# Parking split weights in DRAM as one float32 and splitting them again when they return

## The chip, the core and the metric

One core of a Trainium2 chip runs the kernel; the other cores are not used. The core has TensorE (PE in the profile) for matrix products, VectorE (DVE), ScalarE (ACT) and GpSimd (POOL) for element-wise work, and SyncE (SP), which here issues nearly all DMAs. Each engine takes its instructions strictly in the order in which the program lists them and waits on semaphores where an operand is not ready. Data lie in DRAM, in SBUF (128 partitions) and in PSUM, where TensorE accumulates.

The metric is the device time of one execution in microseconds (us), lower is better. It is measured several times for each kernel, and the median is quoted.

## The reference

A block-sparse attention is followed by a feed-forward layer with softplus:

```python
# q, k, v: (4, 8, 768, 64); w_in: (512, 2048); w_out: (2048, 512); blocks of 32 keys
scores = q @ k.T / sqrt(D)                       # only sampled, neighbour, first and last blocks
attn = softmax(where(mask, scores, -1e9)) @ v
x = attn.transpose(0, 2, 1, 3).reshape(3072, 512)
h = x @ w_in
g = np.maximum(h, 0.0) + np.log1p(np.exp(-np.abs(h)))
out = (g @ w_out).astype(np.float32)
```

The feed-forward weights come as 64-bit floats. The kernel turns each into a float32 with integer work, then into two parts in the `fp32r` format that TensorE multiplies at speed: a high part (the value rounded to that format) and a low part (value minus high part). A product then takes three matmuls: high by high, high by low, low by high.

## The kernel before

The hidden dimension of 2048 is cut into 16 pieces f of 128, and the 3072 tokens into 8 tiles t of 384. One iteration n of the feed-forward works on one pair (t, f). `hidden(n)` runs twelve matmuls of 384 columns into a PSUM tile `h` (lines 235 to 237). ScalarE makes |h| and its exponential (L239, L240), VectorE three steps on `u` and `e` (L246, L248, L249), ScalarE the logarithm (L254), VectorE adds (L259), ScalarE casts the high part `gh` (L263) and VectorE subtracts for the low part `gl` (L269). `project` then runs nine matmuls of 512 columns (L291 to L293), three iterations after the `hidden` of the same n (`LEAD = 3`). Tiles `gh`, `gl`, `e`, `u` have two buffers each.

The work has two phases. In phase 0 the attention runs, and the feed-forward of the first five pieces (`EARLY = 5`, 40 iterations) is spread among its steps; each result goes to DRAM (`yD`), and so does the attention's output, split in two parts (`xD`). In phase 1 the attention is over, and the other eleven pieces run for all tiles (88 iterations); x comes back from `xD`, the partial sums from `yD`.

The weights are converted during phase 0 by the class `Weights`. Its 32 halves are the 16 pieces of `w_in` (which = 0) and of `w_out` (which = 1). `tick()` advances a software pipeline; half number h takes a stage when the tick count is 4h plus the stage's number: load of the raw 64-bit data (SP, L146), magnitude (ACT, L153), last places (ACT, L157), clamp and shift (DVE, L163, L170), assemble (DVE L176, then a POOL addition L180), `high` at 10 (ACT cast, L189), `low` at 12 (DVE subtraction, L193), and `park`: the high part at 12 and the low part at 14. `convert()` calls `tick` between the attention's pieces, at one tick a piece at first and later at half a tick a piece.

The ten halves of the first five pieces stay in SBUF. The other 22 don't fit beside the attention: they are "parked", each as two DRAM tiles of 256 KB (`wD`, L198). When the attention's last piece is done, its SBUF is released and `load_w2` (L893) brings all 44 tiles back through the SP queue, two pieces of the hidden dimension per iteration.

The order on SP is the order of the source. ScalarE, VectorE, GpSimd and TensorE get their order from a list scheduler, which may pull an instruction ahead of its place in the source. At most eight DMAs of the hardware queues are outstanding: each issue first waits for the eighth before it. A load that waits on SP thus holds everything that was listed after it on SP.

Of the kernel before, what the change touches and what calls it, by code (L numbers as in the profile page):

```python
# [8 lines left out]
F32 = mybir.dt.float32  # L9
F32R = mybir.dt.float32r  # L10
# [5 lines left out]
ALU = mybir.AluOpType  # L16
# [11 lines left out]
EARLY = 5  # L28
# [3 lines left out]
LEAD = 3  # L32
# [3 lines left out]
START = 4  # L36

SPREAD = 2

WARM = 50  # L40

# [7 lines left out]
def sparse_attention_ffn(  # L49
# [22 lines left out]
    nc = tc.nc  # L72
    B, NG, P, NP, NI, _ = q.shape
# [4 lines left out]
    NT, DM = out.shape  # L78
    NF = w_in.shape[0]
# [15 lines left out]
    dram = ctx.enter_context(tc.tile_pool(name="dram", bufs=1, space=bass.MemoryType.DRAM))  # L95
# [5 lines left out]
    w1 = ctx.enter_context(tc.tile_pool(name="w1", bufs=1, side="right"))  # L101
    pools = {}
# [5 lines left out]
    xD = [dram.tile([P, 2, NC, TB], F32, name=f"xD{t}") for t in range(NTB)]  # L108
    yD = [dram.tile([P, DM], F32, name=f"yD{n}") for n in range(len(order))]
    wD = {  # L110
        (which, f): [dram.tile([P, DM], F32, name=f"wD{x}{which}{f}") for x in range(2)]
        for f in range(EARLY, NF) for which in range(2)
    }

# [1 line left out]
    W = {}  # L116
    mark = {}

    class Weights:
# [61 lines left out]

        def high(self, h):
            f, which = self.halves[h]
            if f < EARLY:
                W[which, f] = [w1.tile([P, DM], F32R, name=f"w{x}{which}{f}") for x in range(2)]
            else:
                hi = pools["conv"].tile([P, DM], F32R, tag="wh", name=f"wh{which}{f}", bufs=2)
                W[which, f] = [hi, self.t[h].bitcast(F32R)]
            tc.keep_in_program_order(nc.scalar.copy(out=W[which, f][0], in_=self.t[h]))  # L189

        def low(self, h):
            hi, lo = W[self.halves[h][::-1]]
            nc.vector.tensor_tensor(out=lo, in0=self.t[h], in1=hi.bitcast(F32), op=ALU.subtract)  # L193

        def park(self, x, h):
            f, which = self.halves[h]
            if f >= EARLY:
                nc.sync.dma_start(out=wD[which, f][x], in_=W[which, f][x].bitcast(F32))  # L198

        def tick(self):  # L200
            for stage, at in (
                (lambda h: self.park(0, h), 12), (lambda h: self.park(1, h), 14),
                (self.load, 6 - 4 * self.bufs),
                (self.low, 12), (self.high, 10),
                (self.assemble, 3), (self.shift, 2), (self.clamp, 1),
                (self.last_places, 1), (self.magnitude, 0),
            ):
                h, rest = divmod(self.at - at, 4)
                if rest == 0 and 0 <= h < len(self.halves):
                    stage(h)  # L210
            self.at += 1

        def done(self):
            return self.at > 4 * (len(self.halves) - 1) + 14


    X, E, U, L, G, po = {}, {}, {}, {}, {}, {}
# [6 lines left out]
    def load_x(t):  # L224
        x_tile(1, t)
        nc.sync.dma_start(out=X[1, t].bitcast(F32), in_=xD[t])
# [45 lines left out]
    def first_half(j):  # L272
        for stage, n in ((high, j - 2), (logarithm, j - 1), (hidden, j)):
            if 0 <= n < len(seq):
                stage(n)

    def second_half(j):
        for stage, n in ((softplus, j - 1), (low, j - 2), (rounding, j), (project, j - LEAD)):
            if 0 <= n < len(seq):
                stage(n)  # L280
# [18 lines left out]
    def load_y(t):  # L299
        for m in range(GROUPS):  # L300
            Y[t, m] = gp.tile([P, DM], F32, tag="os", name=f"y{t}_{m}", bufs=3)
            nc.sync.dma_start(out=Y[t, m], in_=yD[t * GROUPS + m])
# [49 lines left out]
    for rows in (slice(0, NR * BLOCK), slice(NR * BLOCK, P)):  # L352
# [4 lines left out]
        out=vbuf[0][:, 0, 0, :], out_offset=None, in_=v,  # L357
# [158 lines left out]
    def load_values(m):  # L516
# [18 lines left out]
        if g < 2:  # L535

            for c, lo in enumerate((b * S, (b + 1) * S - BLOCK)):
                i1 = i0 if c == 0 else 0
                if m < SPREAD:
                    if i1 == 0:  # L540
# [311 lines left out]
    def attend():  # L852
        nonlocal done
        attention[done]()
        done += 1
        gather()
        convert()

    SECOND = NTB * EARLY
# [3 lines left out]
    def convert():  # L863

        nonlocal owed
        if done < START:
            return
        owed += EARLY_TICKS if weights.at < 4 * len(early) + 9 else LATE_TICKS
        while owed >= 1 and not weights.done():
            weights.tick()  # L870
            owed -= 1
            if weights.at == 4 * weights.extra + 2:
                extractx.close()
                pools["kv2"] = kv2.enter_context(tc.tile_pool(name="kv2", bufs=1))
# [4 lines left out]
    def due(x):  # L879

        last, at = 0.0, needs[0]
        for t in range(1, NTB):
            end = t * EARLY - AHEAD
            if x <= end:
                return at + (needs[t] - at) * (x - last) / (end - last)
            last, at = end, needs[t]
        return len(attention)

    def load_w2(f):
        for which in range(2):  # L890
            W[which, f] = [pools["w2"].tile([P, DM], F32R, name=f"w{x}{which}{f}") for x in range(2)]
            for x in range(2):
                nc.sync.dma_start(out=W[which, f][x].bitcast(F32), in_=wD[which, f][x])  # L893

    ahead = None
    for j in range(len(seq) + LEAD):
        if j >= SECOND:
            t, f = seq[j][1:] if j < len(seq) else (NTB, -1)
            if f == EARLY + 2 and t + 1 < NTB:
                load_x(t + 1)  # L900
            if f == EARLY + 4:
                load_y(t)
        if j == SECOND - 3:
            load_x(0)
        first_half(j)
        while done < len(attention) and done < due(j + 0.5):
            attend()
        convert()
        second_half(j)
        while done < len(attention) and done < due(j + 1.0):  # L910
            attend()
        convert()
        if done == len(attention) and ahead is None:
            assert weights.done(), weights.at
            actx.close()
            kv2.close()
            pools["w2"] = ctx.enter_context(tc.tile_pool(name="w2", bufs=1, side="right"))
            ahead = EARLY
        while ahead is not None and ahead < min(NF, EARLY + 2 * (j + EARLY - SECOND + 1)):
            load_w2(ahead)  # L920
            ahead += 1


_BLOCKS = 24
# [35 lines left out]
```

## Time and profile before

| | |
|---|---|
| median of 3 runs | 853.09 us (847.7, 853.09, 854.35) |
| the profiled execution's own time | 850.83 us |
| span of its profile | 848.8 us |
| last store of the attention's output (start of the issue on SP) | 444.20 us |
| DMA traffic | HBM read 104.14 MB, written 36.70 MB |
| granted TensorE clock, mean | 0.975 |

The span is the time from the first to the last instruction that the profile shows; the 2 us beside it are start and end of the execution. The attention and phase 0 take about the first 444 us, phase 1 the rest. In the page's rows an engine's busy time is the union of its instructions; a line such as `L189 ACT CAST wh<-wt x22: 601/609/636` gives the source line, the engine, the operation, output and input tile, the count and the shortest, median and longest duration in ns. In a timeline row, square brackets give the time for which the engine sat idle before the instruction and what it waited for. In a row of windows, the stretch is followed by its length and by the busy time of each engine with the count of instructions, then the granted clock, the busy share of the DMA engines and their GB/s.

### The profile page before, as it was taken

How to read it: one execution, taken by the hardware profiler on the slowest of the kernel's cores; microseconds unless marked ns; L12 is line 12 of the kernel's file. 1: busy time of each engine (PE TensorE's matmuls, PEld its weight loads, DVE VectorE, ACT ScalarE, POOL GpSimd, SP SyncE). 2: the span in 40 equal slices, each digit the busy share in tenths (PEclk: the TensorE clock that was granted, in tenths of full speed). 3: DMA queues.
4: the chain of work that ended last, by engine and by line, in shares of the span. 5: the costliest groups of instructions: out<-in, count | busy, mean ns of one | idle time of the engine just before them, and what ended most of it. 6: DMA issues, size and time to landing. Idle time of an engine off the chain costs nothing.

```text
span 848.8 us, 22274 instructions
## 1 busy us (share of the span) xinstructions
PE 811.8 (96%) x8492; PEld 683.7 (81%) x8492; DVE 582.0 (69%) x1473; ACT 486.2 (57%) x1167; POOL 219.4 (26%) x389
## 2 busy tenths in 40 slices
PE   8779899999999899999999999999999999999998
PEld 7657677767778677787789999999999999999996
DVE  4587997787888778877655556556565656565564
ACT  3776776667776667666655544444444444444443
POOL 6582855652545625553000000000000000000000
PEclk9797999999999999998999999999999999999999
DMA  8778598686897877965529923112222203030011
GB/s 254 232 216 310 184 238 273 202 281 198 232 304 237 291 234 203 303 192 189 175 82 379 396 87 112 37 75 75 75 75 75 74 26 125 1 124 27 24 52 38
DMA packets 55323, 142.30 MB, mean 168 GB/s; under 512 B 6256, under 2 KB 6384, under 8 KB 53168
## 3 DMA queue, kind: packets, MB, share of 16 engines
q1 hardware_dynamic: 49216, 122.37, 44.2%
q0 software_dynamic: 5712, 17.57, 7.0%
q8 instruction: 67, 1.10, 0.6%
q10 hardware_dynamic: 288, 0.93, 0.3%
q14 instruction: 40, 0.33, 0.1%
HBM read 104.14 MB, written 36.70 MB: 166 GB/s over the span
## 4 chain that ended last, share of the span: by engine, by line
PE 73%; DVE 10%; ACT 9%; DMA 3%; issue 3%; another core or an unknown queue 1%; SPq 0%; DVEq 0%; ACTq 0%
PE o L291 10%; PE o L292 10%; PE o L293 10%; PE h L235 10%; PE h L236 9%; PE h L237 9%; ACT pr L649 5%; PE x L692 4%; PE s L585 4%; PE t L662 3%; PE s L591 2%; DMA vg<-in_v_dram 2%; PE y L737 1%; ACT pt L669 1%; DVE pr L624 1%
## 5 line engine op out<-in xcount | busy, mean ns | idle before, releaser
L235 PE MATMUL h<-x,w 128*128 128x384 f32 x512 | 176.9, 346 | 1.7 <-DVE nmax L624 1.0
L236 PE MATMUL h<-x,w 128*128 128x384 f32 x512 | 173.1, 338 | 0.0
L237 PE MATMUL h<-x,w 128*128 128x384 f32 x512 | 172.5, 337 | 0.0
L246 DVE TENSOR_SCALAR u<-e 128x384 f32<-128x384 f32 x128 | 49.6, 388 | 168.2 <-ACT e L240 168.1
L291 PE MATMUL o<-w,gh 128*128 128x512 f32 x384 | 156.3, 407 | 0.0
L293 PE MATMUL o<-w,gl 128*128 128x512 f32 x384 | 154.1, 401 | 0.0
L292 PE MATMUL o<-w,gh 128*128 128x512 f32 x384 | 153.7, 400 | 0.0
L649 ACT ACTIVATE pr<-pr,nmax 128x256 f32<-128x256 f32 (+2 forms) x208 | 110.3, 532 | 64.7 <-DVE nmax L599 42.3
L239 ACT ACTIVATE e<-h 128x384 f32<-128x384 f32 x128 | 62.8, 490 | 144.0 <-PE h L237 142.1
L263 ACT CAST gh<-u 128x384 fp32r<-128x384 f32 x128 | 65.7, 513 | 80.7 <-PE o L292 80.6
L235 PEld LDWEIGHTS h<-x,w 128*128 128x128 f32 x512 | 96.7, 189 | 10.5 <-DVE nmax L624 3.1
L550 POOL DMA_INDIRECT vg<-in_v_dram,ix x88 | 88.5, 1005 | 60.8 <-PE x L692 31.5
L494 POOL COPY kg<-kT 128x128 f32 x252 | 85.4, 384 | 59.1 <-PE s L585 53.1
L236 PEld LDWEIGHTS h<-x,w 128*128 128x128 f32 x512 | 96.9, 189 | 4.0
L237 PEld LDWEIGHTS h<-x,w 128*128 128x128 f32 x512 | 96.7, 189 | 0.0
L599 DVE CUSTOM_DVE_ANT_1 pr<-s,mask 128x256 f32<-128x256 f32 (+1 forms) x192 | 69.7, 417 | 28.6 <-PE s L591 16.4
L293 PEld LDWEIGHTS o<-w,gl 128*128 128x128 f32 x384 | 73.2, 191 | 17.5
L292 PEld LDWEIGHTS o<-w,gh 128*128 128x128 f32 x384 | 73.3, 191 | 13.5 <-issue 0.6
L291 PEld LDWEIGHTS o<-w,gh 128*128 128x128 f32 x384 | 73.1, 190 | 13.5 <-issue 0.4
L254 ACT ACTIVATE u<-u 128x384 f32<-128x384 f32 x128 | 67.0, 523 | 24.9 <-DVE e L248 24.9
L269 DVE TENSOR_TENSOR gl<-u,gh 128x384 fp32r<-128x384 f32 x128 | 73.7, 576 | 5.6 <-ACT gh L263 5.6
L248 DVE SCALAR_TENSOR_TENSOR e<-u,e 128x384 f32<-128x384 f32 x128 | 73.0, 570 | 3.9
(81 smaller groups left out, 1147.9 us busy)
## 6 DMA issues: line engine op xcount, KB each, us to landing
vg<-in_v_dram SPq DMA_DIRECT2D x19, 768.0 KB
xD<-x SPq DMA_DIRECT2D x8, 1536.0 KB
x<-xD SPq DMA_DIRECT2D x8, 1536.0 KB
w<-wD SPq DMA_DIRECT2D x44, 256.0 KB
raw<-in_w_in_dram SPq DMA_DIRECT2D x16, 512.0 KB
raw<-in_w_out_dram SPq DMA_DIRECT2D x16, 512.0 KB
qc<-in_q_dram SPq DMA_DIRECT2D x24, 256.0 KB
vg<-in_v_dram SPq DMA_DIRECT2D x12, 512.0 KB
```

Source lines behind the costliest of these rows:

```text
L235: nc.tensor.matmul(ph, wh[:, cols], hi[:, c], start=(c == 0), stop=False)
L236: nc.tensor.matmul(ph, wh[:, cols], lo[:, c], start=False, stop=False)
L237: nc.tensor.matmul(ph, wl[:, cols], hi[:, c], start=False, stop=(c == NC - 1))
L248: nc.vector.scalar_tensor_tensor(out=e, in0=u, scalar=-1.0, in1=e, op0=ALU.add, op1=ALU.subtract)
L269: nc.vector.tensor_tensor(out=gl, in0=l, in1=G[n].bitcast(F32), op=ALU.subtract)
L291: nc.tensor.matmul(po[m], gh[:, cols], wh, start=first, stop=False)
L292: nc.tensor.matmul(po[m], gh[:, cols], wl, start=False, stop=False)
L293: nc.tensor.matmul(po[m], gl[:, cols], wh, start=False, stop=last)
L494: copy(out=kd[:, i, NR + s, :], in_=kT[b][:, bass.ds(x, 1), :].rearrange("p n f -> p (n f)"))
L550: nc.gpsimd.indirect_dma_start(out=vd[0 : 3 * BLOCK, 1, i, :], out_offset=None, in_=v, in_offset=bass.IndirectOffsetOnAxis(ap=ix[:, b, 4 * ...
L599: nc.vector.tensor_tensor_reduce(out=pr[r][rows, j], in0=ps[r][rows, j], in1=mask[rows, g].unsqueeze(2).to_broadcast([ni * BLOCK, NS, BLOCK]),
L649: nc.scalar.activation(x, x, AF.Exp, bias=nmax[rows, r, j : j + 1], scale=-1.0, accum_out=rs[rows, h : h + 1])
```

## The change

A half that is to be parked stops after `assemble`. Its single float32 tile `wt` goes to DRAM at tick 8 (`PARK = 8`); the cast of line 189 and the subtraction of line 193 are made only for the ten halves that stay, and the `wh` tiles (two buffers) go away. 44 stores become 22, and 44 loads become 22. In phase 1 `load_w2` brings each half into the buffer of its low part, and a new function `split_w2` casts it into the high part on ScalarE and subtracts in place on GpSimd. In the source the split of a half stands three iterations ahead of the matmuls that use it.

```diff
+PARK = 8
...
-        (which, f): [dram.tile([P, DM], F32, name=f"wD{x}{which}{f}") for x in range(2)]
+        (which, f): dram.tile([P, DM], F32, name=f"wD{which}{f}")
...
         def high(self, h):
             f, which = self.halves[h]
-            if f < EARLY:
-                W[which, f] = [w1.tile([P, DM], F32R, name=f"w{x}{which}{f}") for x in range(2)]
-            else:
-                hi = pools["conv"].tile([P, DM], F32R, tag="wh", name=f"wh{which}{f}", bufs=2)
-                W[which, f] = [hi, self.t[h].bitcast(F32R)]
+            if f >= EARLY:
+                return
+            W[which, f] = [w1.tile([P, DM], F32R, name=f"w{x}{which}{f}") for x in range(2)]
...
-        def park(self, x, h):
+        def park(self, h):
             f, which = self.halves[h]
             if f >= EARLY:
-                nc.sync.dma_start(out=wD[which, f][x], in_=W[which, f][x].bitcast(F32))
+                nc.sync.dma_start(out=wD[which, f], in_=self.t[h])
...
-                (lambda h: self.park(0, h), 12), (lambda h: self.park(1, h), 14),
-                (self.load, 6 - 4 * self.bufs),
+                (self.park, PARK), (self.load, 6 - 4 * self.bufs),
...
     def load_w2(f):
         for which in range(2):
             W[which, f] = [pools["w2"].tile([P, DM], F32R, name=f"w{x}{which}{f}") for x in range(2)]
-            for x in range(2):
-                nc.sync.dma_start(out=W[which, f][x].bitcast(F32), in_=wD[which, f][x])
+            nc.sync.dma_start(out=W[which, f][1].bitcast(F32), in_=wD[which, f])
+
+    def split_w2(f, which):
+
+        hi, lo = W[which, f]
+        nc.scalar.copy(out=hi, in_=lo.bitcast(F32))
+        nc.gpsimd.tensor_tensor(out=lo, in0=lo.bitcast(F32), in1=hi.bitcast(F32), op=ALU.subtract)
...
+        for which in range(2):
+            f = EARLY + j + 3 - SECOND - LEAD * which
+            if EARLY <= f < NF:
+                split_w2(f, which)
```

The scheduler doesn't leave the splits where the source has them. On ScalarE, at the change of phases, the row before runs from the logarithm of iteration 35 to the first step of iteration 38. `e` and `u` are tiles of the softplus with the iteration's number behind them, `os` are partial sums on their way to `yD`:

```order
L254 ACTIVATE u35_7165<-u35_7165 128x384
L239 ACTIVATE e36_7210<-h36_7197 128x384
L240 ACTIVATE e36_7210<-e36_7210 128x384
L263 CAST gh35_7247<-u35_7165 128x384
L254 ACTIVATE u36_7216<-u36_7216 128x384
L239 ACTIVATE e37_7263<-h37_7250 128x384
L240 ACTIVATE e37_7263<-e37_7263 128x384
```

After the change the same stretch reads as follows; a tile `w005` is the high part (0) of `w_in` (0), piece 5, and `w105` its low part, into which the load goes:

```order
L899 CAST w005_7068<-w105_7069 128x512
L899 CAST w015_7071<-w115_7072 128x512
L241 ACTIVATE e36_7096<-h36_7083 128x384
L899 CAST w006_7074<-w106_7075 128x512
L242 ACTIVATE e36_7096<-e36_7096 128x384
L899 CAST w016_7077<-w116_7078 128x512
L265 CAST gh35_7129<-u35_7055 128x384
L899 CAST w007_7115<-w107_7116 128x512
L256 ACTIVATE u36_7102<-u36_7102 128x384
L899 CAST w017_7118<-w117_7119 128x512
L899 CAST w008_7121<-w108_7122 128x512
L241 ACTIVATE e37_7145<-h37_7132 128x384
```

Eight casts (an eighth follows behind the last row) stand in less than two iterations, up to five of them within one, directly behind the loads that bring their data. The other fourteen stand in the same manner from just ahead of iteration 39's first step to iteration 41's logarithm. GpSimd has no other work left by then, so its row is the 22 subtractions, in the order of the casts; it ended with the attention's gathers before:

```order
L552 DMA vg1_176<-in_v_dram,ix_157 96x512 x2
L900 TENSOR_TENSOR w105_7069<-w105_7069,w005_7068 128x512
L900 TENSOR_TENSOR w115_7072<-w115_7072,w015_7071 128x512
L900 TENSOR_TENSOR w106_7075<-w106_7075,w006_7074 128x512
L900 TENSOR_TENSOR w116_7078<-w116_7078,w016_7077 128x512
```

In phase 0 the two operations vanish from their engines and little else moves. On ScalarE, for a half in mid-phase, the row before was this (`pr` are the attention's exponentials, `x` is the attention's output tile):

```order
L157 ACTIVATE raw19_3201<-raw19_3201 128x512
L189 CAST wh18_3832<-wt18_3299 128x512
L263 CAST gh12_3883<-u12_3602 128x384
L751 CAST x0_3_3166<-y13_3840 128x4x64
L649 ACTIVATE pr30_0_3797,sums30_3835<-pr30_0_3797,nmax30_3796 128x256 x2
```

The second of these five rows is gone after the change, and the cast of `gh12` follows directly; the subtraction into `wt18` is gone from VectorE in the same way.

More of the change, by code (lines that the diff above doesn't have):

```diff
@@ L183, in high @@
             f, which = self.halves[h]
-            if f < EARLY:
-                W[which, f] = [w1.tile([P, DM], F32R, name=f"w{x}{which}{f}") for x in range(2)]
-            else:
-                hi = pools["conv"].tile([P, DM], F32R, tag="wh", name=f"wh{which}{f}", bufs=2)
-                W[which, f] = [hi, self.t[h].bitcast(F32R)]
+            if f >= EARLY:
+                return
+            W[which, f] = [w1.tile([P, DM], F32R, name=f"w{x}{which}{f}") for x in range(2)]
             tc.keep_in_program_order(nc.scalar.copy(out=W[which, f][0], in_=self.t[h]))
         def low(self, h):
-            hi, lo = W[self.halves[h][::-1]]
-            nc.vector.tensor_tensor(out=lo, in0=self.t[h], in1=hi.bitcast(F32), op=ALU.subtract)
-        def park(self, x, h):
             f, which = self.halves[h]
             if f >= EARLY:
-                nc.sync.dma_start(out=wD[which, f][x], in_=W[which, f][x].bitcast(F32))
+                return
+            hi, lo = W[which, f]
+            nc.vector.tensor_tensor(out=lo, in0=self.t[h], in1=hi.bitcast(F32), op=ALU.subtract)
+        def park(self, h):
+            f, which = self.halves[h]
+            if f >= EARLY:
+                nc.sync.dma_start(out=wD[which, f], in_=self.t[h])
         def tick(self):
             for stage, at in (
-                (lambda h: self.park(0, h), 12), (lambda h: self.park(1, h), 14),
-                (self.load, 6 - 4 * self.bufs),
+                (self.park, PARK), (self.load, 6 - 4 * self.bufs),
                 (self.low, 12), (self.high, 10),
@@ L213, in done @@
         def done(self):
-            return self.at > 4 * (len(self.halves) - 1) + 14
+            return self.at > 4 * (len(self.halves) - 1) + 12
     X, E, U, L, G, po = {}, {}, {}, {}, {}, {}
@@ L891, in load_w2 @@
             W[which, f] = [pools["w2"].tile([P, DM], F32R, name=f"w{x}{which}{f}") for x in range(2)]
-            for x in range(2):
-                nc.sync.dma_start(out=W[which, f][x].bitcast(F32), in_=wD[which, f][x])
+            nc.sync.dma_start(out=W[which, f][1].bitcast(F32), in_=wD[which, f])
+    def split_w2(f, which):
+        hi, lo = W[which, f]
+        nc.scalar.copy(out=hi, in_=lo.bitcast(F32))
+        nc.gpsimd.tensor_tensor(out=lo, in0=lo.bitcast(F32), in1=hi.bitcast(F32), op=ALU.subtract)
     ahead = None
```

## The prediction

> **What bounds the kernel now.** I read the page first (span, busy time, the chain), then the busy time by windows, to see which engine sets the pace in each phase.
>
> ```profile
> span 848.8 us, 22274 instructions
> PE 73%; DVE 10%; ACT 9%; DMA 3%; issue 3%; another core or an unknown queue 1%; SPq 0%; DVEq 0%; ACTq 0%
> ...
> core 0: us, PE busy (x) PEld busy (x) DVE busy (x) ACT busy (x) POOL busy (x), PEclk, DMA share, GB/s
> 130.00:440.00 310.00, 294.75 (x4640) 233.32 (x4639) 239.60 (x666) 209.06 (x556) 138.99 (x236) 0.98 0.73 228
> 440.00:500.00 60.00, 60.00 (x303) 53.83 (x302) 35.10 (x73) 29.90 (x62) 0.00 (x0) 1.00 0.83 311
> 500.00:542.10 42.10, 42.10 (x212) 38.01 (x211) 25.71 (x53) 19.75 (x41) 0.00 (x0) 1.00 0.22 76
> 386.00:397.00 11.00, 10.85 (x126) 8.91 (x126) 6.32 (x16) 5.95 (x16) 1.78 (x2) 0.69 0.68 229
> ```
>
> From 130 to 440 us, where the parked halves are made, three engines are close to full: TensorE idles 15.25 us of 310, VectorE is busy 77%, ScalarE 67%. The chain runs through VectorE and ScalarE for about a fifth of the whole span, so here a lighter VectorE can move the end. The clock of 0.98 there means another 6 us of TensorE's time lost; the last row shows where one such loss sits. From 440 us on TensorE is full at full clock, ScalarE has half its time free, GpSimd does nothing. Phase 1 is bound by TensorE, and a gain there is excluded; only a loss is possible.
>
> **Removed in phase 0.** The rows of the tiles `wh` and `wt` price the two operations and their neighbours:
>
> ```profile
> L189 ACT CAST wh<-wt x22: 601/609/636, 131.7 to 430.4; 128x512 fp32r<-128x512 f32 x22
> L193 DVE TENSOR_TENSOR wt<-wt,wh x22: 639/693/1994, 133.4 to 431.0; 128x512 fp32r<-128x512 f32 x22
> L180 POOL TENSOR_TENSOR wt<-wt,raw x20: 1294/1306/1595, 131.7 to 399.2; 128x512 int32<-128x512 int32 x20
> ...
> SPq L532 <- PE x L692: 122.1, 16, 13.0
> SPq L198 <- ACT wh L189: 27.9, 5, 11.5
> ```
>
> 22 casts at 0.609 us are 13.4 us of ScalarE, 22 subtractions at 0.693 us are 15.2 us of VectorE, but not all of that lies on the path. What does can be read in the chain, where eight of the 44 stand:
>
> ```profile
> 179.50 0.52 ACT wh L189
> 194.98 0.60 DVE wt L193
> 208.84 0.52 ACT wh L189
> 209.38 0.52 DVE wt L193
> 262.47 0.67 DVE wt L193
> 277.34 0.51 ACT wh L189
> 304.55 0.53 ACT wh L189
> 403.63 0.60 DVE wt L193
> ...
> 296.35 6.60 DMA wD<-wh
> ```
>
> Their sum is 4.47 us. Two bounds: nothing, if at each place another chain is as long (the eight are spread, and TensorE is busy beside them); and 15.25 + 6 = 21 us, if TensorE never waited nor lost its clock again. I take 4.5 us, the direct count, because a shorter chain is partly replaced by its neighbour while a lighter queue also shortens waits that the chain doesn't name; I let these two cancel. The 6.60 us put down to a store of `wh` I don't count: the ScalarE instruction that it released stood directly behind another one, so little was waited for.
>
> The queues: SP issues 22 stores fewer. Five times a store held SP for the cast, 27.9 us in all (the row above), with loads for the attention listed behind it; a store at tick 8 waits for an addition five ticks older, so this wait ends. TensorE hardly waited for these loads, so it is worth nothing beyond the 4.5. Late next on SP are the buffers that TensorE frees, 122.1 us in the row above it. VectorE's pressure from the additions L180 stays.
>
> **Moved in phase 1: loads.** 22 loads of 256 KB vanish. TensorE waited for none (60.00 busy of 60.00), so the saving is nothing, and the cover is TensorE's own work. The loads that stay start as before, behind the attention's last store:
>
> ```profile
> 444.20 0.32 SPq L758 DMA_DIRECT2D xD<-x  x1
> 444.99 12.22 SPq L893 DMA_DIRECT2D w<-wD  x16
> 457.63 0.32 SPq L226 DMA_DIRECT2D x<-xD  x1
> 461.20 20.55 SPq L893 DMA_DIRECT2D w<-wD  x28
> ```
>
> Sixteen issues take 12.22 us, 0.76 each, so the eight that stay ahead of x take 6 us and x comes some 6 us sooner. The remaining fourteen follow the three stores of `os`, about as before, over 11 us instead of 20.55.
>
> **Added: casts.** 22 times 0.609 us on ScalarE, which needs 19.75 / 10 = 1.98 us of each iteration of 4.21 us. Five in one iteration are 3.05 us against 2.23 us free: it falls 0.8 us behind, and a little more where a cast waits for its load with everything on ScalarE queued behind it. Whether that reaches TensorE depends on the reserve, read from one iteration of VectorE and the end of a `hidden` two iterations on:
>
> ```profile
> 488.18 0.36 DVE L246 TENSOR_SCALAR u<-e 128x384 f32<-128x384 f32 x1 [1.73 <-ACT e L240]
> 488.58 0.56 DVE L248 SCALAR_TENSOR_TENSOR e<-u,e 128x384 f32<-128x384 f32 x1
> 489.17 0.56 DVE L249 SCALAR_TENSOR_TENSOR e<-h,e 128x384 f32<-128x384 f32 x1
> 489.64 0.55 DVE L269 TENSOR_TENSOR gl<-u,gh 128x384 fp32r<-128x384 f32 x1
> 490.11 0.55 DVE L259 TENSOR_TENSOR u<-u,e 128x384 f32<-128x384 f32 x1
> 492.39 0.36 DVE L246 TENSOR_SCALAR u<-e 128x384 f32<-128x384 f32 x1 [1.73 <-ACT e L240]
> ...
> 495.51 0.49 ACT L239 ACTIVATE e<-h 128x384 f32<-128x384 f32 x1 [1.40 <-PE h L237]
> ```
>
> The low part `gl` is done at 489.64 + 0.55 = 490.19; the `hidden` after which its `project` runs ends at 495.51. So both engines together may fall about 5.3 us behind before TensorE stops. The casts alone don't: I cost them at nothing. If that cover is used up by something else, each us counts.
>
> **Added: subtractions on GpSimd.** The nearest row is the addition L180: same shape, same engine, 1.306 us. 22 of them are 28.7 us. Two scenes show what such an operation does to VectorE:
>
> ```profile
> 246.70 0.92 POOL L550 DMA_INDIRECT vg<-in_v_dram,ix  x1 [0.30 <-issue]
> 247.26 2.10 DVE L248 SCALAR_TENSOR_TENSOR e<-u,e 128x384 f32<-128x384 f32 x1
> 247.63 1.30 POOL L180 TENSOR_TENSOR wt<-wt,raw 128x512 int32<-128x512 int32 x1
> ...
> 302.97 0.56 DVE L248 SCALAR_TENSOR_TENSOR e<-u,e 128x384 f32<-128x384 f32 x1
> 303.18 1.51 POOL L180 TENSOR_TENSOR wt<-wt,raw 128x512 int32<-128x512 int32 x1 [5.74 <-ACT raw L157]
> 303.56 0.56 DVE L249 SCALAR_TENSOR_TENSOR e<-h,e 128x384 f32<-128x384 f32 x1
> ```
>
> At 247.26 an operation of 0.56 us took 2.10: it ended 0.43 us after L180, as if it had begun only then. At 302.97 VectorE was first, and L180 took 0.2 us longer. L249, which reads `h` from PSUM, ran beside L180 unhurt. So the two exclude each other, except for L249. Of an iteration's five operations, four can be shut out.
>
> Now the sum. The casts deliver the subtractions in two bursts, eight from about 452 us, fourteen from about 466. If VectorE gets one operation of 0.55 us in between two subtractions, the second burst lasts 14 x (1.31 + 0.55) = 26 us, 6.2 iterations. It shuts VectorE out for 18.3 us, against 6.2 x 1.73 = 10.7 us of idle time: 7.6 us behind, or 4.1 if L249 always runs beside a subtraction. The first burst gives by the same steps 10.5 - 6.1 = 4.4, or 2.4. Together 6.5 to 12.0 us; less the reserve of 5.3, TensorE loses 1.2 to 6.7 us. I take 4, the middle. The ends for the range: nothing, where subtractions fall into idle time; 28.7 - 5.3 = 23 us, where none does.
>
> The Trainium skill, SBUF — State Buffer, section "SBUF: two separate sides", has a rule for this: VectorE and GpSimd share one pair of ports as an exclusive lock, and "whichever" of the two starts first keeps it for the whole instruction. By that rule alternation is what happens, and the sum would be the 4 us. The scene at 303 agrees; the scene at 247 doesn't: VectorE had started 0.37 us earlier and lost. What differs is that GpSimd came there directly from another instruction.
>
> **The sum.** 850.83 (the profiled execution) - 4.5 + 4 = 850.3. The median of the runs shown, 853.09, is 2.3 above that execution, with runs on both sides of it; I add half, which gives 851.5.
>
> **The rivals.**
>
> *The splits hide, and phase 0 gains more.* For it: GpSimd is idle and VectorE has 1.73 us free per iteration from 440 us on; and 28.6 us of work leave two engines that stand on the path, far more than the eight pieces of the chain. Against it: bursts of five casts an iteration. Price: -4.5 to half of the bound of 21, -10.5, with no loss: 841.5 to 847.5.
>
> *GpSimd keeps the port within a burst* (the other side, slower). For it: the scene at 247, where a waiting VectorE operation lost to a GpSimd operation queued directly behind another; in a burst every subtraction stands like that. Against it: after each L180 shown, VectorE went on at once, though never with a second L180 behind it. It decides once subtractions queue, that is when casts come faster than one per 1.31 us. Price: the first burst shuts VectorE out for 10.5 us less 2.5 x 1.73 idle, 6.2; the second 18.3 less 4.3 x 1.73, 10.8; less 1.2 regained between and the reserve of 5.3: 10.5 us. That gives 858; if the clock falls once as at 386 us (11 us at 0.69, 3.4 us lost), 861.
>
> *No effect.* The eight chain pieces are replaced by equal ones, and the splits hide: 852. For it: TensorE is busy 95% even in phase 0.
>
> **How the numbers follow.** The forecast (alternation, 847 to 857): 0.42. The splits hide: 0.30. GpSimd keeps the port: 0.17. No effect: 0.11. A measurement of this kernel tells about 1% from no change, 844.6 and 861.6. Below the first lies half of the second case and a little of the forecast, 0.19; above the other some half of the third and a tail of the forecast, 0.12; between them 0.69. The range from 843 to 860 leaves out about one in ten on each side; it doesn't reach the bound of 23 us, for which no subtraction may meet idle time.
>
> **What would show it.** Phase 0: the last store of `xD`, at 444.20 us before, starts 3 to 6 us earlier; rows `wh` vanish; the wait of L198 for the cast is gone. If it starts no earlier, the first term was wrong. Phase 1: 22 POOL rows of about 1.3 us, VectorE operations of 1.5 to 2 us between 452 and 500 us, TensorE idle there about 4 us in sum, at full clock. No such idle time means the first rival; VectorE operations of 2.5 us or more, waiting through two subtractions, mean the second. A cast that waits over 5 us for its load would be a cause that I have costed at nothing.

## The result, and the profile after

The change made the kernel slower by half a per cent: 854.63 us in the median of 20 runs (850.39 to 856.57) against 849.86 of 20 runs before (845.03 to 854.35). The ratio is 1.0053 with a 95% interval of 1.0037 to 1.0069, 4.5 us. The forecast of 851.5 us had stood against a median of 853.09 from three runs; with 17 more runs that median fell by 3 us, and from 849.86 the same sum (-4.5 + 4) would have given 849.4.

Two things moved, in opposite directions. The first is the end of the attention. The rows of SP in the timeline after the change, to be held beside those of before, with start and length in us:

```profile
437.44 0.32 SPq L760 DMA_DIRECT2D xD<-x  x1
438.23 5.68 SPq L894 DMA_DIRECT2D w<-wD  x8
444.33 0.32 SPq L228 DMA_DIRECT2D x<-xD  x1
455.08 7.27 SPq L894 DMA_DIRECT2D w<-wD  x14
```

The last store of the attention's output starts 6.8 us earlier in this execution (437.44 for 444.20), and the loads follow as forecast: eight before x, fourteen later, 0.5 to 0.7 us each. The second is phase 1. From that store to the end of the span it took 848.8 - 444.2 = 404.6 us before and 851.6 - 437.4 = 414.2 us now, 9.6 us more. The windows of the changed kernel show where, in the same columns as before:

```profile
437.44:476.00 38.56, 38.30 (x192) 34.27 (x191) 31.02 (x38) 26.46 (x55) 25.97 (x18) 1.00 0.79 293
476.00:484.00 8.00, 1.90 (x8) 1.10 (x7) 7.93 (x8) 3.79 (x8) 6.66 (x5) 0.84 0.09 33
484.00:492.00 8.00, 8.00 (x30) 7.02 (x31) 4.72 (x11) 3.01 (x8) 0.00 (x0) 0.73 0.49 164
492.00:500.00 8.00, 8.00 (x42) 7.18 (x41) 4.44 (x10) 3.51 (x8) 0.00 (x0) 1.00 0.00 0
```

TensorE is full until 476 us and again from 484 us on. Between them it has 1.90 us of work in 8, VectorE is full (7.93) and GpSimd nearly; and in the next 8 us the granted clock is 0.73. After 492 us TensorE is full at full clock again. Narrower windows show when the clock was lowered:

```profile
481.50:483.73 2.23, 0.00 (x0) 0.00 (x0) 2.20 (x4) 0.62 (x2) 1.16 (x1) 0.50 0.00 0
483.73:488.37 4.64, 4.64 (x13) 4.07 (x13) 3.76 (x8) 1.74 (x4) 0.00 (x0) 0.50 0.74 246
```

It fell to 0.50 while TensorE stood, and TensorE then worked 4.64 us at it. What TensorE waited for is in the table of waits from 430 to 530 us (total, times, longest):

```profile
PE o L293 <- DVE os L312: 3.6, 1, 3.6
PE o L293 <- ACT os L312: 2.5, 1, 2.5
PE o L295 <- DVE gl L271: 0.3, 1, 0.3
```

It waited 6.1 us for two copies `os` and almost nothing for a low part `gl`. A copy `os` moves a finished PSUM tile of phase 0 to SBUF; there are three such PSUM tiles, so each third of the first `project` of phase 1 waits for one copy of the last tile of phase 0. The rows of the weight tiles show the new operations, with shortest, median and longest duration in ns:

```profile
L899 ACT CAST w<-w x22: 604/610/622, 445.3 to 474.8; 128x512 fp32r<-128x512 f32 x22
L900 POOL TENSOR_TENSOR w<-w,w x22: 1293/1582/1625, 446.0 to 481.3; 128x512 fp32r<-128x512 f32 x22
```

In GpSimd's timeline they stand in two bursts without a gap, 8 and 14:

```profile
445.99 11.58 POOL L900 TENSOR_TENSOR w<-w,w 128x512 fp32r<-128x512 f32 x8 [33.95 <-DMA w<-wD]
461.61 21.05 POOL L900 TENSOR_TENSOR w<-w,w 128x512 fp32r<-128x512 f32 x14 [4.05 <-ACT w L899]
```

VectorE's timeline, in one iteration of the second burst and at the place of the wait, and below it the two matmuls of TensorE that waited, with start and length in us:

```profile
468.01 1.45 DVE L248 TENSOR_SCALAR u<-e 128x384 f32<-128x384 f32 x1
469.50 1.54 DVE L250 SCALAR_TENSOR_TENSOR e<-u,e 128x384 f32<-128x384 f32 x1
471.07 0.56 DVE L251 SCALAR_TENSOR_TENSOR e<-h,e 128x384 f32<-128x384 f32 x1
471.54 1.06 DVE L271 TENSOR_TENSOR gl<-u,gh 128x384 fp32r<-128x384 f32 x1
472.53 1.64 DVE L261 TENSOR_TENSOR u<-u,e 128x384 f32<-128x384 f32 x1
474.09 1.45 DVE L248 TENSOR_SCALAR u<-e 128x384 f32<-128x384 f32 x1
...
481.58 1.50 DVE L250 SCALAR_TENSOR_TENSOR e<-u,e 128x384 f32<-128x384 f32 x1
483.00 0.68 DVE L312 COPY os<-o 128x512 f32<-128x512 f32 x1
...
479.12 0.50 PE L293 MATMUL o<-w,gh 128*128 128x512 f32 x1 [2.46 <-ACT os L312]
483.73 0.80 PE L293 MATMUL o<-w,gh 128*128 128x512 f32 x1 [3.64 <-DVE os L312]
```

Operations of 0.36 and 0.56 us take 1.06 to 1.64; the one that reads PSUM, L251, stays at 0.56. An iteration lasts 474.09 - 468.01 = 6.08 us on VectorE where TensorE needs 4.21. The second burst covers about three such iterations (their first steps start at 462.89, 468.01, 474.09 and 480.12); after them the copy at 483.00 is late, and TensorE stands.

### The profile page after: what moved, and what is told of

Its sections match the earlier page's. It is cut to its first block, busy times and chain, and to the rows that moved or that the text cites. A ratio compares the mean times of both kernels' runs of the same rounds, so it can differ in the third digit from the quotient of the medians.

```text
span 851.6 us, 22232 instructions
## 1 busy us (share of the span) xinstructions
PE 810.5 (95%) x8492; PEld 683.3 (80%) x8492; DVE 583.3 (68%) x1451; ACT 484.4 (57%) x1167; POOL 252.9 (30%) x411
## 4 chain that ended last, share of the span: by engine, by line
PE 76%; DVE 10%; ACT 9%; issue 4%; another core or an unknown queue 0%; POOL 0%; DVEq 0%; ACTq 0%; POOLq 0%
PE h L237 10%; PE o L293 10%; PE o L294 10%; PE h L238 10%; PE h L239 10%; PE o L295 10%; ACT pr L651 4%; PE x L694 4%; PE t L664 4%; PE s L587 3%; PE s L593 2%; PE warm L823 2%; DVE e L250 1%; PE y L739 1%; DVE u L248 1%
## 5 line engine op out<-in xcount | busy, mean ns | idle before, releaser
L248 DVE TENSOR_SCALAR u<-e 128x384 f32<-128x384 f32 x128 | 54.8, 428 | 164.8 <-ACT e L242 164.8
L294 PEld LDWEIGHTS o<-w,gh 128*128 128x128 f32 x384 | 73.2, 191 | 13.4 <-issue 0.6
L250 DVE SCALAR_TENSOR_TENSOR e<-u,e 128x384 f32<-128x384 f32 x128 | 79.0, 617 | 3.9
L261 DVE TENSOR_TENSOR u<-u,e 128x384 f32<-128x384 f32 x128 | 77.1, 603 | 1.5 <-ACT u L256 0.3
```

What stands on the lines that cost most here:

```text
L250: nc.vector.scalar_tensor_tensor(out=e, in0=u, scalar=-1.0, in1=e, op0=ALU.add, op1=ALU.subtract)
L261: nc.vector.tensor_tensor(out=l, in0=l, in1=e, op=ALU.add)
L294: nc.tensor.matmul(po[m], gh[:, cols], wl, start=False, stop=False)
```

## The experiments

All ratios are against the kernel before, run on the same chip at the same time, with a 95% interval. The first four ran on a chip where the kernel before takes 835.43 us; the others on chips with 850 us. "Phase 1" is the time from the start of the last store of `xD` to the end of the span, read from each profile.

**Without the subtractions**, on the 835 us chip, and again later on one with 850 us:

```diff
-        nc.gpsimd.tensor_tensor(out=lo, in0=lo.bitcast(F32), in1=hi.bitcast(F32), op=ALU.subtract)
```

> The changed kernel without the 22 subtractions on GpSimd in phase 1; the low parts keep the whole value. Casts, loads and phase 0 stay. If the loss in phase 1 comes from the port that GpSimd and VectorE share, it goes: phase 0 ends about 7 us earlier than in the kernel before, TensorE has no idle time from 440 to 500 us, and the time is 849.9 - 6.8 = 843 us (ratio 0.992). If the 22 casts on ScalarE cause the loss, it stays at 854 us (1.005). If the earlier end of phase 0 is an accident of one profile, 850 us (1.000).

826.08 us, ratio 0.9894 (0.9866 to 0.9922); phase 1 took 824.0 - 418.8 = 405.2 us, with no wait of TensorE. So the casts and the changed loads cost at most the 0.6 us by which this exceeds the old 404.6, and 414.2 - 405.2 = 9.0 of the 9.6 us go with the subtractions.

**Splits spread, subtraction on VectorE**: both calls wrapped so that they keep their place in the source's order.

```diff
-        nc.scalar.copy(out=hi, in_=lo.bitcast(F32))
-        nc.gpsimd.tensor_tensor(out=lo, in0=lo.bitcast(F32), in1=hi.bitcast(F32), op=ALU.subtract)
+        tc.keep_in_program_order(nc.scalar.copy(out=hi, in_=lo.bitcast(F32)))
+        tc.keep_in_program_order(nc.vector.tensor_tensor(out=lo, in0=lo.bitcast(F32), in1=hi.bitcast(F32), op=ALU.subtract))
```

> The changed kernel with the subtractions on VectorE, and casts and subtractions pinned at their places in the source: one split an iteration for three iterations, then two. VectorE needs 2.41 + 2 x 0.6 = 3.6 us of an iteration of 4.21, ScalarE 1.98 + 2 x 0.61 = 3.2 us. If the port is the cause: no idle time of TensorE in phase 1, 843 to 845 us (0.992 to 0.994). If added element-wise work as such is the cause, whichever engine does it: 850 us or more (1.000 and above).

827.86 us, ratio 0.9915 (0.9890 to 0.9940); phase 1 405.2 us.

**Splits spread, subtraction on GpSimd**: the same with `nc.gpsimd`.

> The changed kernel with casts and GpSimd subtractions pinned at their places in the source, at most two an iteration in place of five in a burst. The profile of the change shows VectorE and GpSimd alternating, 1.53 us for a pair; two pairs and the two other port operations take 3.06 + 1.1 = 4.2 us, just an iteration of 4.21. If the bursts are the cause: 843 to 846 us (0.992 to 0.996). If the 22 subtractions cost the same wherever they stand: 854 us (1.005).

826.11 us, ratio 0.9894 (0.9864 to 0.9925); phase 1 404.9 us. The same 22 subtractions on the same engine cost nothing when the order gives each iteration at most two. The window of this run over the stretch of the splits, and below it pieces of the timelines of VectorE and GpSimd there:

```profile
419.10:500.00 80.90, 80.90 (x406) 73.08 (x405) 62.24 (x97) 49.95 (x103) 33.23 (x22) 1.00 0.49 179
```

```profile
455.58 0.68 DVE L312 COPY os<-o 128x512 f32<-128x512 f32 x1
...
460.21 1.53 DVE L250 SCALAR_TENSOR_TENSOR e<-u,e 128x384 f32<-128x384 f32 x1
461.78 0.56 DVE L251 SCALAR_TENSOR_TENSOR e<-h,e 128x384 f32<-128x384 f32 x1
462.25 1.06 DVE L271 TENSOR_TENSOR gl<-u,gh 128x384 fp32r<-128x384 f32 x1
463.24 0.55 DVE L261 TENSOR_TENSOR u<-u,e 128x384 f32<-128x384 f32 x1
...
457.09 5.81 POOL L900 TENSOR_TENSOR w<-w,w 128x512 fp32r<-128x512 f32 x4 [2.91 <-ACT w L899]
```

The single operations are stretched as much as in the burst (1.53 us at L250), but between them others run free (0.55), and TensorE is busy 80.90 of 80.90 us. In time four subtractions once ran without a gap (5.81 us from 457.09), just behind the copy `os` of the change of tiles, which had ended at 456.26. So the run shows that spreading helps; it doesn't separate how many stand together from where they stand, ahead of that copy or behind it.

**The old kernel with 22 subtractions added**:

```diff
+        for which in range(2):
+            f = EARLY + j + 3 - SECOND - LEAD * which
+            if EARLY <= f < NF:
+                hi, lo = W[which, f]
+                scratch = pools["w2"].tile([P, DM], F32, tag="scratch", name=f"scr{which}{f}", bufs=2)
+                nc.gpsimd.tensor_tensor(out=scratch, in0=lo.bitcast(F32), in1=hi.bitcast(F32), op=ALU.subtract)
```

> The kernel before with 22 added GpSimd subtractions of 128x512 in phase 1, from the loaded high and low parts into a scratch tile that nothing reads; phase 0 is untouched and no cast is added. If the shared port is the cause of the loss in phase 1: about 6 us of idle time of TensorE and some of a lower clock, 856 to 862 us (1.007 to 1.014). If the casts or the loads are: 850 us (1.000).

842.0 us, ratio 1.0083 (1.0047 to 1.0118); phase 1 411.4 us, 6.8 more than 404.6. The waits of TensorE in this run:

```profile
PE o L291 <- DVE os L310: 3.7, 1, 3.7
PE o L291 <- ACT os L310: 0.4, 1, 0.4
```

The wait is for the same copies, here under their old line number, and the clock falls to 0.70 for 8 us behind it. With no cast, no changed load and no changed phase 0, the subtractions alone make a loss, 6.8 of the 9.6 us, at the same place.

**The change again**, unaltered, for comparison on another chip.

> The changed kernel, unaltered, beside the next three on one chip. Phase 0 ends 7 to 13 us earlier than in a kernel whose phase 0 is the old one, phase 1 (from the last store of xD to the end) takes 9 to 10 us more than the 404.6 of the kernel before. Ratio 0.997 to 1.006, the more above 1 the smaller the gain of phase 0 on that chip.

855.49 us, ratio 1.0066 (1.0047 to 1.0086); phase 1 414.2 us, with waits of 3.7, 2.5 and 0.2 us as in the first profile. The ratio lies just above the range expected: phase 0 gained about 4 us here (worked out below), not 7 or more.

**The middle copy on ScalarE**, on the same chip as the last run:

```diff
-                (nc.vector.tensor_copy if m % 2 else nc.scalar.copy)(out=os_, in_=po[m])
+                (nc.vector.tensor_copy if m % 2 and t < NTB - 1 else nc.scalar.copy)(out=os_, in_=po[m])
```

> The changed kernel with one edit: the middle copy of the last tile of phase 0 from PSUM (os022) stands on ScalarE instead of VectorE. In the changed kernel TensorE waited 2.5 us for the first copy and 3.6 us for this one, 0.3 us for gl. If the reserve fails at the change of tiles, where the copies stand behind the late VectorE, the second wait goes, phase 1 takes 405 + 5 to 6 us instead of 414, and the ratio to the kernel before is 0.004 to 0.007 below that of the unaltered change. If the late low parts gl are what stops TensorE, the wait moves to gl and the time stays within 1 us of the unaltered change.

849.45 us, ratio 1.0000 (0.9978 to 1.0023), 0.0066 below the unaltered change; phase 1 409.7 us. Its waits:

```profile
PE o L293 <- ACT os L312: 2.5, 1, 2.5
PE o L295 <- DVE gl L271: 0.2, 1, 0.2
```

Moving one copy of 0.6 us out of VectorE's queue takes away the 3.7 us wait; bursts, casts and subtractions are unchanged. The wait for the first copy, on ScalarE, and the short one for `gl` stay. That the first copy is late for the same reason was not tried by a run; in the profile of the change it starts at 478.50, behind a logarithm that had waited 1.75 us for VectorE.

**No subtraction in phase 0** (the first edit below alone), then **no split in phase 0, with 44 stores and loads** (both edits):

```diff
         def low(self, h):
+            if self.halves[h][0] >= EARLY:
+                return
...
-                hi = pools["conv"].tile([P, DM], F32R, tag="wh", name=f"wh{which}{f}", bufs=2)
-                W[which, f] = [hi, self.t[h].bitcast(F32R)]
+                W[which, f] = [self.t[h].bitcast(F32R)] * 2
+                return
```

> The kernel before without the 22 subtractions on VectorE in phase 0; the casts and the 44 stores and loads stay, the low parts keep the whole value. By the chain of the kernel before these were 2.4 of 4.5 us; phase 0 of the change gained 7 to 13. If VectorE is what bounds phase 0: at least half of that gain, ratio 0.988 to 0.995. If the gain comes from the stores that vanish: 1.000.

> The kernel before without the 22 casts and the 22 subtractions in phase 0; the single tile is stored twice and 44 tiles are loaded, so the DMA traffic is the old one, and the products of phase 1 lack the split. If the element-wise work makes the gain: phase 0 as short as in the change, ratio 0.985 to 0.992. If the 22 stores that vanish make it: 1.000, or little below e7.

849.52 us, ratio 1.0004 (0.9989 to 1.0020), and 850.06 us, ratio 0.9991 (0.9972 to 1.0010). Both expectations that gave the work the whole gain failed: taking 13.4 us off ScalarE and 15.2 us off VectorE saves about 1 us in the middle and at most 2.4 by the interval.

**One store a half**, the work of phase 0 kept:

```diff
-            if f >= EARLY:
+            if f >= EARLY and x:
                 nc.sync.dma_start(out=wD[which, f][x], in_=W[which, f][x].bitcast(F32))
...
-                nc.sync.dma_start(out=W[which, f][x].bitcast(F32), in_=wD[which, f][x])
+                nc.sync.dma_start(out=W[which, f][x].bitcast(F32), in_=wD[which, f][1])
```

> The kernel before with the casts and subtractions of phase 0 kept, but only the low part stored, at its old place (tick 14); phase 1 loads that tile for both parts, 44 loads as before, so its products lack the high part. If the 22 stores that vanish make phase 0 of the change shorter: 4 to 9 us faster, ratio 0.990 to 0.995. If they don't: 1.000, and what remains is the place of the store or the three edits together.

852.42 us, ratio 1.0027 (1.0008 to 1.0045). Against both expectations it is a little slower; the stores alone don't make the gain either.

**The spread change again, and with the store at tick 14**:

```diff
-PARK = 8
+PARK = 14
...
-            return self.at > 4 * (len(self.halves) - 1) + 12
+            return self.at > 4 * (len(self.halves) - 1) + 14
```

> The changed kernel with the splits pinned at their places in the source, as in the third experiment, again. Ratio 0.989 to 0.996, by what phase 0 gains on this chip; phase 1 takes 405 us.

> The same with the store of a parked half at tick 14 in place of 8, where the low part was stored before. If it matters that the store is early (the tile wt is free six ticks sooner, SP meets the store sooner): 2 us or more slower than at tick 8. If only the number of stores and the work matter: within 1 us of it.

846.48 us, ratio 0.9950 (0.9932 to 0.9969), and 846.35 us, ratio 0.9955 (0.9932 to 0.9977). Where the store stands makes no difference. Phase 1 took 404.9 us in both.

**The subtractions on VectorE in a burst** (`nc.gpsimd` replaced by `nc.vector`, nothing pinned):

> The changed kernel with the 22 subtractions on VectorE, not pinned: the scheduler puts up to six of them into one iteration. 22 x 0.6 = 13 us of VectorE in place of 22 x 1.53 in which it gets one operation. If the alternation with GpSimd is what costs: VectorE falls behind by about 2 us in a burst and TensorE doesn't wait, phase 1 takes 405 to 406 us. If any burst of element-wise work behind which the os copies stand costs as much: 410 us or more.

847.33 us, ratio 0.9963 (0.9935 to 0.9990); phase 1 405.2 us, no wait of TensorE. On VectorE itself the same work, in bursts around the same copies, does no harm (0.68 us an operation there); on GpSimd, where it shuts VectorE out, it does.

**Both edits of phase 0 together** (no split and one store a half, 44 loads), the work alone, and the change without subtractions, on one chip:

> The kernel before without the casts and subtractions of phase 0, and with one store a half (tick 14) in place of two; phase 1 loads that tile for both parts, 44 loads, and its products lack the split. Phase 0 does the work of the change. If the gain needs both, the lighter engines and the 22 stores fewer: as much as the spread change gained here, 0.994 to 0.996, and 2 us or more below e14. If the stores add nothing: the same as e14.

> The same with two stores a half, as in e8, on the same chip as e13: 0.997 to 1.001, as before, if the first measurement holds.

> The changed kernel without the GpSimd subtractions, as in e1, beside these two. Phase 0 is that of the change, phase 1 takes 405 us: 0.994 to 0.996 on a chip like that of e10, 0.989 on one like that of e1. As far as the 22 loads fewer do nothing, it equals e13.

847.70 us, ratio 0.9966 (0.9942 to 0.9991); 850.05 us, 0.9985 (0.9962 to 1.0007); 845.94 us, 0.9954 (0.9926 to 0.9981). The middle values are ordered as the edits add up, but the intervals overlap. Held directly against each other, both without the split, the 12 runs with 22 stores are 1.9 us shorter in the mean than the 12 with 44 (95% interval 0.4 to 3.3).

## Why the prediction was wrong, point by point

**Phase 0, -4.5 us: right in size by luck, wrong in its reading.** On the chips with 850 us the ratios give, after taking out what phase 1 changed, (1.0066 - 1) x 850.2 - 9.6 = -4.0 us (the change again) and (0.9950 - 1) x 850 - 0.3 = -4.6 us (spread). On the 835 us chip it is 0.0106 x 835.4 + 0.3 = 9.2 us. The 6.8 us of the one profile are no measure: this start differs by 5 us between the two profiles with splits spread on the slower chips (439.63 and 444.43) whose medians agree. The count of chain pieces came out by luck: those were pieces of the casts and subtractions, and without these alone the kernel gained about 1 us. Work and stores together gave 0.0034 x 850.5 = 2.9 us. That both are needed is suggested, not settled: the stores alone made the kernel slower.

Part of this gain is clock, which I had only in an upper bound. Each run's mean granted clock is on record, and its time multiplied by (1 - clock) estimates what a lowered clock cost it. Averaged over the runs of one chip, that is 17.7 us for the kernel before and 14.7 for the spread change there: 3.0 of the 3.4 us between their mean times. With the work alone taken away (two stores a half, last chip) the clock costs 21.3 us against 18.6, which eats most of the 2.9 us saved otherwise. On the 835 us chip it is 15.5 against 10.9, half of the gain of the spread change. The two profiles whose starts differ by 5 us have clocks of 0.984 and 0.977, 6.0 us by the same estimate. What lowers the clock in phase 0, and why the other half of the gain on the 835 us chip is larger than elsewhere, is open.

**Loads and casts at nothing: right within 0.6 us.** That is all by which phase 1 without the subtractions exceeds the old one.

**Alternation of VectorE and GpSimd: right.** Neither starved: between two subtractions VectorE got one operation, every 1.5 us, and L251 with its PSUM operand ran beside them. This is the case that the rule of the Trainium skill (SBUF — State Buffer, "SBUF: two separate sides") leads to, and the trace of the change agrees with it; the scene at 247 us, where an operation took 2.10 us, stays unexplained. The rival in which GpSimd keeps the port is out: no operation of VectorE took longer than 1.65 us. The delay was estimated at 6.5 to 12.0 us; counted from the attention's last store, the copy ends after 483.68 - 437.44 = 46.2 us in place of 37.1, so 9.1 us late. The parts were rougher than the sum: a pair takes 1.52 us (6.08 / 4), not 1.86, and the second burst 21 us, not 26.

**The reserve of 5.3 us: the step that failed.** I took it from `gl` in an ordinary iteration, and TensorE hardly waited for `gl` (0.3 us, for the `gl` that ended 35.2 us after the attention's last store in place of 29.8). At the change of tiles another chain is shorter. In the timeline of the kernel before, the rows are:

```profile
480.64 0.68 DVE L310 COPY os<-o 128x512 f32<-128x512 f32 x1
...
483.40 0.39 PE L291 MATMUL o<-w,gh 128*128 128x512 f32 x1
```

The copy ends at 481.32 and the matmul that overwrites its PSUM tile starts at 483.40, 2.1 us later. With that in place of 5.3 my own delay of 6.5 to 12.0 gives 4.4 to 9.9 us of idle time in place of the 4 that I forecast, and 6.4 was measured. The copies stand in VectorE's and ScalarE's queues behind everything that is late; that they were on this path was in the trace, and I looked only at the steady iteration. The 5.3 us would have been overrun too, one iteration later, but by less: the next `gl` was ready at 478.65, and TensorE, which stopped at about 476.5, would have needed it at about 477, some 1.7 us sooner (an estimate from the starts of the matmuls).

**The clock: costed only in a rival.** I wrote that TensorE would idle at full clock. It stood for 2.5 and 3.6 us close together, and then worked 4.64 us at a clock of 0.50, which costs half of that, 2.3 us. Of the 9.6 us, 6.4 are waits and 2.3 the clock. The remaining 0.9 isn't accounted for; the runs without any wait differ by as much among themselves (404.5 to 405.4).

So the sum was -4.5 + 4, a little faster, and came out as about -5 + 9.6: 4.5 us slower. The term that turned the sign is the loss in phase 1, mis-sized by the reserve first and the clock second.

## What to carry to other kernels

Work moved to an idle engine isn't free where that engine and one on the path shut each other out, as GpSimd and VectorE did here; what counts is where its operations gather: in two bursts, the second just ahead of the change of tiles, they cost 9.0 us, and pinned at two an iteration in the order they cost nothing, which made the same change 0.5 to 1.1% faster than the kernel before. Read the reserve of a pipeline at the place where its buffers turn over (here the last tile of a phase), not in the steady iteration. And look at the built order: the source had the splits spread, and the scheduler gathered them behind their loads.

## What the runs showed of the hardware

Under contention both engines lengthen: the subtraction took 1.293 us at best and 1.582 in the median, which fits its waiting for VectorE's operation in turn; a pair of one subtraction and one VectorE operation takes 1.52 us. TensorE's granted clock fell to 0.50 during waits of 2.5 and 3.6 us and stayed there until 488.4 us, 4.6 us after work went on. The same kernel took 835.43 us on one chip and 850 on others. The old phase 0 was shorter there (in the run with 22 subtractions added, the last store of the attention's output starts at 430.30 us, where the first profile has 444.20); phase 1 took 404.5 to 405.4 us on both, in every run in which TensorE did not wait.
